# A new issue order, other engines for some copies and another warm-up table, in a recurrence followed by two dense layers

## The chip, the cores and the metric

One core of a Trainium2 chip runs the kernel. The metric is the device time of one execution in microseconds. Three runs of the kernel before gave 346.52, 346.58 and 348.45 us; the median is 346.58 us.

In the profile PE is TensorE (matmuls; PEld is its weight loads), DVE is VectorE, ACT is ScalarE, POOL is GpSimd, and SP is the engine that issues all transfers from memory.

## The reference

A recurrence over 768 positions (2 batches, 8 heads of 48 channels), then two dense layers:

```
for t in range(S):
    cur = einsum(u * k_t, v_t)                  # 48 x 48 per head
    y[t] = einsum(r_t, state + cur)
    state = w_t * state + einsum(k_t, v_t)
x = y as (2, 768, 384)
h = relu(x @ w_in)                              # 384 -> 1024
x = (h * sigmoid(conv over 3 positions of h)) @ w_out
out = x + relu(layernorm(x) @ w_ch1) @ w_ch2    # 384 -> 1536 -> 384
```

All data are float32; the weights arrive as 64-bit floats and are converted in the kernel.

## The kernel before

**Stages.** The recurrence is cut into 12 chunks of 64 positions. For chunk c the steps are:

- transfers `load_pk`, `load_kr`, `load_v` (decay, keys and queries, values);
- DVE scans `pa1` (L447) and `pa2` (L464) with a reciprocal `par` (L455) between them; the products `pak` (kd, L459) and `pa3` (xr, L475), on DVE or POOL; `pa5`, `bo1` on ACT;
- TensorE step `p1` (a_ps, kdn_ps), its copies `bo4` (bb, L514, ACT), `k2` (kdn, L479) and the masked product `bo5` (db, L517, DVE or POOL);
- TensorE step `p2`, then `a2` (db, L530, DVE), then TensorE step `p3` (y_ps, st_ps; it reads the values);
- `s2` (L548, DVE) and `s3` (ss, L479) update the state that `p2` of the next chunk reads; `y2` (L579, ACT) and `y3` (L583, DVE) copy the output away into xh, as a high and a low part; `p2` of the next chunk waits for `y3` as well.

Each p step is 32 to 64 small matmuls with as many weight loads.

The first dense layer works on four blocks i of 192 positions. `y4(i)` moves some rows of xh by DMA; `h1(i,f)` is 9 matmuls for one of 8 column groups f; ACT, DVE and POOL apply relu, convolution (`g2`, L635, two DVE instructions for each f) and gate (`g6p` on DVE or POOL); `o1(i,t,part)` is 6 matmuls for the second product. Block 0 can start when `y3(3)` and `y4(0)` are done. The last layer (`m1x`, `n1`) follows in three groups.

Weights are converted beside this: `vl` loads, `va` (ACT, L751) and twice `vc` (DVE, L761 and L766) build the float, `vh` and `vlo` split it into two parts. The last layer has `wl`, `wa`, `wc`, `wh`, `wlo`.

**What sets the order.** `PLACE` gives each of some 1,250 steps a number; steps are issued in that order, and each engine takes its own in that order and waits at the first that isn't ready. `ENGINE` says by a letter for each instance which engine does a step that can run on two (V is DVE, P is POOL, A is ACT). `WARM` puts matmuls without use (L957) ahead of the step with that number: `{10: 13}` puts 13 ahead of number 10. What each step computes is the same in both kernels.

```
for k in sorted(steps, key=place.get):
    if place[k] in WARM:
        order.append(("warm", WARM[place[k]]))
    order.append(k)
```

Of the kernel before, what the change touches and what calls it, by code (L numbers as in the profile page):

```python
# [48 lines left out]
    'init': (1,),  # L49
    'init_p': (0, 12),  # L50
    'load_cst': (7,),
    'load_cw': (82,),
    'load_gln': (125,),
    'top_a': (309,),
    'top_v': (429,),
    'conv_cw': (95,),
    'load_kr': (4, 19, 30),
    'load_pk': (2, 9, 29, 52, 91, 116, 163, 222, 278, 336, 384, 422),
# [50 lines left out]
    'free_attention': (525,),  # L109
    'wl': (531, 535, 554, 567, 583, 611, 631, 642, 659, 671, 688, 725, 729, 760, 782, 821, 841, 856, 876, 889,  # L110
        897, 909, 938, 956),
    'wa': (536, 549, 562, 579, 605, 621, 636, 655, 674, 693, 706, 732, 746, 805, 827, 835, 854, 864, 886, 895,
        915, 929, 952, 964),
    'wc': (541, 548, 555, 556, 571, 572, 581, 586, 612, 615, 629, 630, 640, 650, 657, 663, 675, 683, 696, 702,
        710, 719, 736, 742, 768, 772, 806, 817, 832, 833, 847, 849, 855, 860, 874, 875, 887, 892, 896, 906, 920,
        921, 940, 945, 953, 958, 970, 973),
# [1146 lines left out]
```

## Time and profile before

| | before |
|---|---|
| median of 3 runs | 346.58 us |
| profiled execution, its own time | 347.53 us |
| span of the profiled execution | 345.7 us |
| TensorE busy / VectorE busy / ScalarE busy / GpSimd busy | 318.4 / 216.9 / 252.4 / 117.2 us |
| mean granted TensorE clock | 0.968 |

The span runs from the first to the last instruction of one execution; its own time is 1.8 us longer. Busy shares are means over stages, so a stage is read on its own: by the busy time of each engine in it, and by what ended the waits in it.

### The profile page before, as it was taken

How to read it: one execution, taken by the hardware profiler on the slowest of the kernel's cores; microseconds unless marked ns; L12 is line 12 of the kernel's file. 1: busy time of each engine (PE TensorE's matmuls, PEld its weight loads, DVE VectorE, ACT ScalarE, POOL GpSimd, SP SyncE). 2: the span in 40 equal slices, each digit the busy share in tenths (PEclk: the TensorE clock that was granted, in tenths of full speed). 3: DMA queues.
4: the chain of work that ended last, by engine and by line, in shares of the span. 5: the costliest groups of instructions: out<-in, count | busy, mean ns of one | idle time of the engine just before them, and what ended most of it. 6: DMA issues, size and time to landing. Idle time of an engine off the chain costs nothing.

```text
span 345.7 us, 9057 instructions
## 1 busy us (share of the span) xinstructions
PE 318.4 (92%) x3611; PEld 284.7 (82%) x3619; DVE 216.9 (63%) x433; ACT 252.4 (73%) x664; POOL 117.2 (34%) x124
## 2 busy tenths in 40 slices
PE   7474697988999999999999999999999999999994
PEld 3453666868999889999988889899888999988994
DVE  7796799997998869988997837732423302142011
ACT  3463449987859466998998989867697868585960
POOL 3443438888448564497743211200000000000000
PEclk9969579999999999999999999999999999999998
DMA  7864668374144304544411433316546464363541
GB/s 236 329 238 144 236 187 276 101 266 131 36 156 144 84 2 138 137 141 126 138 46 50 134 92 92 93 46 166 155 109 173 133 203 121 75 196 88 177 114 37
DMA packets 16845, 47.91 MB, mean 139 GB/s; under 512 B 2720, under 2 KB 4512, under 8 KB 16800
## 3 DMA queue, kind: packets, MB, share of 16 engines
q1 hardware_dynamic: 16800, 47.31, 44.3%
q8 instruction: 29, 0.48, 0.6%
q14 instruction: 16, 0.13, 0.1%
HBM read 43.75 MB, written 2.36 MB: 133 GB/s over the span
## 4 chain that ended last, share of the span: by engine, by line
PE 61%; DVE 18%; ACT 7%; issue 6%; POOL 4%; DMA 2%; SPq 0%; ACTq 0%; DVEq 0%; POOLq 0%
PE h_ps L907 22%; PE o_b L924 11%; PE o_a L924 11%; DVE h_ps L635 5%; PE o_b L679 4%; PE h_ps L614 3%; PE a_ps L484 2%; PE y_ps L540 2%; PE o_a L679 2%; PE y_ps L525 2%; DVE stf L766 1%; DVE q L447 1%; DVE pp L464 1%; DMA pk<-in_pk 1%; ACT h_ps L632 1%
## 5 line engine op out<-in xcount | busy, mean ns | idle before, releaser
L907 PE MATMUL h_ps<-xh,w_s 128*128 128x512 f32 x324 | 79.0, 396 | 0.0
L907 PEld LDWEIGHTS h_ps<-xh,w_s 128*128 128x128 f32 x324 | 60.3, 188 | 12.4
L614 PE MATMUL h_ps<-xh,win_s 128*128 128x388 f32 x288 | 57.1, 345 | 1.3 <-ACT z L660 1.0
L614 PEld LDWEIGHTS h_ps<-xh,win_s 128*128 128x128 f32 x288 | 50.0, 188 | 3.8 <-ACT z L660 3.1
L635 DVE SCALAR_TENSOR_TENSOR h_ps<-h,cw_sb,h_ps 128x384 f32<-128x384 f32 x64 | 39.1, 614 | 3.4 <-ACT h_ps L632 2.3
L663 POOL TENSOR_TENSOR z<-z,h 128x384 f32<-128x384 f32 x32 | 32.6, 1021 | 22.4 <-ACT z L660 22.2
L916 DVE SCALAR_TENSOR_TENSOR win_s<-h_ps,win_s 128x512 fp32r<-128x512 f32 x18 | 12.4, 689 | 34.2 <-ACT win_s L913 34.2
L916 DVE SCALAR_TENSOR_TENSOR wout_s<-h_ps,wout_s 128x512 fp32r<-128x512 f32 x18 | 12.2, 689 | 28.6 <-ACT wout_s L913 28.5
L679 PE MATMUL o_b<-wout_s,gs 128*128 128x384 f32 x144 | 29.2, 342 | 0.0
L679 PE MATMUL o_a<-wout_s,gs 128*128 128x384 f32 x144 | 28.6, 340 | 0.0
L773 POOL TENSOR_TENSOR w_s<-stf,w_s 128x384 fp32r<-128x384 f32 x17 | 17.4, 1029 | 31.4 <-ACT w_s L770 21.8
L679 PEld LDWEIGHTS o_b<-wout_s,gs 128*128 128x128 f32 x144 | 25.0, 188 | 0.6
L679 PEld LDWEIGHTS o_a<-wout_s,gs 128*128 128x128 f32 x144 | 25.0, 188 | 0.4
L671 POOL TENSOR_TENSOR gs<-z,gs 128x384 fp32r<-128x384 f32 x20 | 20.7, 1038 | 13.3 <-ACT gs L667 13.2
L924 PE MATMUL o_b<-w_s,wout_s 128*128 128x384 f32 x108 | 20.8, 339 | 0.0
L924 PE MATMUL o_a<-w_s,win_s 128*128 128x384 f32 x108 | 20.7, 338 | 0.0
L924 PE MATMUL o_b<-w_s,win_s 128*128 128x384 f32 x108 | 20.5, 338 | 0.0
L660 ACT ACTIVATE z<-h_ps 128x384 f32<-128x384 f32 x32 | 15.8, 492 | 6.5 <-DVE h_ps L635 3.4
L924 PE MATMUL o_a<-w_s,wout_s 128*128 128x384 f32 x108 | 20.4, 339 | 0.0
L913 ACT ACTIVATE win_s<-h_ps 128x512 fp32r<-128x512 f32 x18 | 10.8, 599 | 13.2 <-PE h_ps L907 10.6
L507 PE MATMUL kdn_ps<-ident,kd 48*64 48x48 f32 x352 | 14.3, 232 | 6.4 <-issue 5.1
L459 POOL TENSOR_TENSOR kd<-pk,q 112x512 f32<-112x512 f32 x9 | 11.9, 1322 | 23.7 <-DVE q L447 11.4
(120 smaller groups left out, 730.4 us busy)
## 6 DMA issues: line engine op xcount, KB each, us to landing
stg<-in_w SPq DMA_DIRECT2D x36, 384.0 KB, 3.1
pk<-in_pk SPq DMA_DIRECT2D x9, 800.0 KB, 4.5
vs<-in_vn SPq DMA_DIRECT2D x12, 384.0 KB, 6.0
stg<-in_win SPq DMA_DIRECT2D x4, 768.0 KB, 7.2
stg<-in_wout SPq DMA_DIRECT2D x4, 768.0 KB, 5.6
stg<-in_win SPq DMA_DIRECT2D x8, 384.0 KB, 3.2
stg<-in_wout SPq DMA_DIRECT2D x8, 384.0 KB, 3.3
stg<-in_wf SPq DMA_DIRECT2D x6, 384.0 KB, 3.4
```

The costliest lines, as they stand in the source:

```text
L459: eng.tensor_mul(kd, gx(pk_t[c][0:112, KO:KO + 512], C), gx(q_t[c][:, 1:521], 65)[:, :, 1:65])
L507: PE.matmul(kp[lo:lo + 64, g, :], kd[lo:lo + 48, g, :], ident[lo:lo + 48, lo:lo + 48], start=True, stop=True)
L614: PE.matmul(hv, win_s[:, wa, m, kt, fs], x[:, kt, xa, :, 0:NX[i]], start=(k == 0), stop=(k == 8))
L635: V.scalar_tensor_tensor(out=z3(zp(i, f)), in0=tap(i, f, j), scalar=cw_sb[:, f, j:j + 1], in1=z3(zp(i, f)), op0=ALU.mult, op1=ALU.add)
L660: A.activation(z, zp(i, f), AF.Sigmoid)
L663: P.tensor_mul(z3(z_t[i, f]), z3(z_t[i, f]), tap(i, f, 1))
L671: eng.tensor_sub(gs[:, 1], z_t[i, f], _as_f32(gs[:, 0]))
L679: PE.matmul(op, g_t[i, f][:, ga, t * 128:(t + 1) * 128], wout_s[:, wa, f // 2, f % 2, :], start=(f == 0 and k == 0), stop=(f == MF - 1 and ...
L773: eng.tensor_sub(lo, f_t[key], _as_f32(hi))
L907: PE.matmul(hp, late["w1"][:, wa, m // 2, kt, (m % 2) * 128:(m % 2 + 1) * 128], xt(gr)[:, xa, kt].rearrange("p a t -> p (a t)"), start=(k ...
L916: V.scalar_tensor_tensor(out=h2s(m)[:, 1], in0=hp2_t[m], scalar=0.0, in1=_as_f32(h2s(m)[:, 0]), op0=ALU.max, op1=ALU.subtract)
L924: PE.matmul(op2_t[t], h2s(m)[:, ga, t * 128:(t + 1) * 128], late["w2"][:, wa, m // 2, m % 2, :], start=(m == 0 and k == 0), stop=(m == MF2 ...
```

## The change

The same steps with the same operands are issued in another order (`PLACE`), some instances change their engine (`ENGINE`), and the useless matmuls stand elsewhere and are 60 instead of 41 (`WARM`). The table of the pk buffers is filled beforehand, so that `load_kr` of a chunk may stand ahead of its `load_pk`.

```diff
-    'load_v': (20, 49, 83, 97, 124, 188, 273, 274, 386, 400, 423, 485),
+    'load_v': (23, 46, 73, 89, 153, 180, 229, 254, 321, 344, 434, 456),
...
-    'a2': (25, 59, 84, 108, 150, 224, 272, 321, 396, 450, 482, 513),
+    'a2': (28, 61, 92, 118, 159, 231, 282, 332, 405, 447, 481, 520),
...
-ENGINE = {'pak': 'PVPPPPVPPPVP',
-          'pa3': 'VPPPPPPPPPPP',
-          'bo1': 'AAAAAAAAAAAA',
-          'bo5': 'PPVVVPPPVVPP',
-          'k2': 'AVAAAAAAAAV',
-          's3': 'AAAVAAAAAAA',
-          'vlo': 'PPPPVPPV',
-          'g6p': 'PPPVPVVVVVVPPPVPPPPVPPPPPPVPVPVP',
-          'wlo': 'PVVPPPPPPPPPPVVPPPPVVPPV'}
...
-WARM = {10: 13, 55: 2, 60: 5, 85: 1, 107: 1, 111: 1, 143: 12, 202: 2, 266: 4}
+ENGINE = {'pak': 'VPPPPPPPVVPP',
+          'pa3': 'VVPPPPPPPPPP',
+          'bo1': 'AAAAAAAAAVAA',
+          'bo5': 'VPVPVPPVPPPP',
+          'k2': 'VAAAAAAVAAA',
+          's3': 'AAVAAAAVVAV',
+          'vlo': 'PPPPVPVP',
+          'g6p': 'VPPPPVPPPVPPPPPPPPPPPPPPVPVPPPPP',
+          'wlo': 'PVPPPPVPPPPVPPPPPPPPPVPV'}
...
+WARM = {15: 10, 37: 12, 44: 2, 58: 3, 85: 4, 96: 7, 113: 2, 123: 1, 144: 10, 157: 5, 211: 4}
...
-    pk_t = {}
+    pk_t = {c: pk_bufs[c % 2] for c in range(NCH)}
...
-        t = pk_t[c] = pk_bufs[c % 2]
+        t = pk_t[c]
```

Three places of the order are shown. The first is VectorE between `a2(2)` and `a2(3)`: from the two `vc` that follow `a2(2)` to `a2(3)` (L530) in the kernel before.

```order
L761 SCALAR_TENSOR_TENSOR o_b<-stg,o_b 128x384
L766 SCALAR_TENSOR_TENSOR stf<-stg,o_b 128x384
L548 TENSOR_TENSOR st_ps<-st_ps,wt 112x384
L790 TENSOR_SCALAR o_b<-cw_raw 128x24
L792 SCALAR_TENSOR_TENSOR o_b<-cw_raw,o_b 128x24
L793 SCALAR_TENSOR_TENSOR o_b<-cw_raw,o_b 128x24
L794 COPY cw_sb<-o_b 128x24
L583 TENSOR_TENSOR xh<-y_ps,xh 112x2x4x64
L583 TENSOR_TENSOR xh<-y_ps,xh 112x2x4
L517 TENSOR_TENSOR db_101<-bb,msk 128x512
L447 SCALAR_TENSOR_TENSOR q<-pk_98,ind 112x521
L530 COPY_PREDICATED db_101<-msk,a_ps 128x512
```

The same stretch of VectorE in the changed kernel, from the first instruction after `a2(2)` to `a2(3)`:

```order
L447 SCALAR_TENSOR_TENSOR q<-pk_98,ind 112x521
L761 SCALAR_TENSOR_TENSOR o_b<-stg,o_b 128x384
L548 TENSOR_TENSOR st_ps<-st_ps,wt 112x384
L766 SCALAR_TENSOR_TENSOR stf<-stg,o_b 128x384
L583 TENSOR_TENSOR xh<-y_ps,xh 112x2x4x64
L583 TENSOR_TENSOR xh<-y_ps,xh 112x2x4
L479 COPY ss<-st_ps 112x384
L455 RECIPROCAL d_0_102<-q 112x8
L761 SCALAR_TENSOR_TENSOR o_b<-stg,o_b 128x384
L766 SCALAR_TENSOR_TENSOR stf<-stg,o_b 128x384
L530 COPY_PREDICATED db_101<-msk,a_ps 128x512
```

The masked product `bo5(3)` (L517), which waits for ScalarE's copy of `p1(3)`, has left VectorE for GpSimd; the copy `s3(2)` has come, `pa1(4)` stands first instead of last, and two more `vc` stand ahead of `a2(3)`; the four small instructions of `conv_cw` stand earlier, ahead of `a2(2)`.

The second place is VectorE between `a2(3)` and the end of `y3(3)`, before:

```order
L455 RECIPROCAL d_0_102<-q 112x8
L761 SCALAR_TENSOR_TENSOR o_b<-stg,o_b 128x384
L464 SCALAR_TENSOR_TENSOR pp<-pk_98,d_0_102 112x520
L766 SCALAR_TENSOR_TENSOR stf<-stg,o_b 128x384
L583 TENSOR_TENSOR xh<-y_ps,xh 112x2x4x2
L583 TENSOR_TENSOR xh<-y_ps,xh 112x2x4x64
```

And in the changed kernel:

```order
L464 SCALAR_TENSOR_TENSOR pp<-pk_98,d_0_102 112x520
L761 SCALAR_TENSOR_TENSOR o_b<-stg,o_b 128x384
L766 SCALAR_TENSOR_TENSOR stf<-stg,o_b 128x384
L583 TENSOR_TENSOR xh<-y_ps,xh 112x2x4x2
L583 TENSOR_TENSOR xh<-y_ps,xh 112x2x4x64
```

Only `par(4)` has left the stretch; the two `vc` now belong to a later weight tile.

The third place is SP's queue of transfers, from the second chunk's `load_pk` on, before:

```order
L429 DMA pk1_99<-in_pk 128x522
L432 DMA pk1_99<-in_pk 128x1024
L435 DMA vs0_96<-in_vn 128x768
L737 DMA stg_221<-in_win 128x768
L429 DMA pk0_98<-in_pk 128x522
L432 DMA pk0_98<-in_pk 128x1024
L435 DMA vs1_97<-in_vn 128x768
```

And in the changed kernel:

```order
L429 DMA pk1_99<-in_pk 128x522
L432 DMA pk1_99<-in_pk 128x1024
L737 DMA stg_129<-in_win 128x768
L432 DMA pk0_98<-in_pk 128x1024
L429 DMA pk0_98<-in_pk 128x522
L435 DMA vs0_96<-in_vn 128x768
L783 DMA cw_raw_218<-in_cw 128x24
```

The values of the first chunk (vs0) are issued after a weight tile and after chunk 2's two parts of pk0, instead of ahead of them.

## Rows read from the trace of the kernel before

**Rows 1.** Page, part 1: busy us (share of span) xinstructions of each engine.

```profile
PE 318.4 (92%) x3611; PEld 284.7 (82%) x3619; DVE 216.9 (63%) x433; ACT 252.4 (73%) x664; POOL 117.2 (34%) x124
```

**Rows 2.** Page, part 2: tenths busy, and granted clock, in 40 equal slices of 8.64 us.

```profile
PE   7474697988999999999999999999999999999994
...
DVE  7796799997998869988997837732423302142011
...
PEclk9969579999999999999999999999999999999998
```

**Rows 3.** Busy us of each engine in five stretches, then granted clock, DMA share, GB/s.

```profile
0.00:43.62 43.62, 27.06 (x818) 20.21 (x823) 32.77 (x60) 19.43 (x51) 17.76 (x20) 0.80 0.66 234
43.62:72.98 29.36, 26.08 (x476) 20.18 (x475) 29.01 (x49) 24.57 (x59) 19.81 (x22) 0.94 0.64 203
72.98:81.63 8.65, 6.94 (x268) 6.17 (x268) 7.39 (x14) 6.14 (x17) 6.99 (x7) 1.00 0.49 168
81.63:340.85 259.22, 258.13 (x2061) 238.02 (x2053) 146.56 (x309) 202.22 (x541) 72.60 (x77) 1.00 0.40 116
340.85:345.70 4.85, 0.19 (x2) 0.09 (x2) 1.21 (x5) 0.00 (x0) 0.00 (x0) 0.82 0.15 49
```

**Rows 4.** VectorE in order of time, 5 to 46 us: start, us, instruction, [idle before <-releaser].

```profile
6.48 1.49 DVE L475 TENSOR_TENSOR xr<-pk,pp 112x512 f32<-112x512 f32 x1
...
10.54 0.72 DVE L530 COPY_PREDICATED db<-msk,a_ps 128x512 f32<-128x512 uint32 x1 [1.42 <-POOL db L517]
...
17.26 0.56 DVE L479 COPY kdn<-kdn_ps 128x384 f32<-128x384 f32 x1 [0.99 <-PE a_ps L484]
...
34.50 0.69 DVE L517 TENSOR_TENSOR db<-bb,msk 128x512 f32<-128x512 f32 x1 [2.64 <-ACT bb L514]
...
42.85 0.77 DVE L583 TENSOR_TENSOR xh<-y_ps,xh 112x16 fp32r<-112x16 f32 x2 [1.78 <-ACT xh L579]
```

**Rows 5.** Chain of waits, 0 to 50 us: start, us, what; TensorE's own breaks.

```profile
14.16 2.31 issue
...
26.51 0.66 issue
...
30.29 2.81 issue
...
38.96 2.06 issue
```

**Rows 6.** Page, part 3: DMA queue, kind, packets, MB, share of 16 engines.

```profile
q8 instruction: 29, 0.48, 0.6%
```

**Rows 7.** DMA queues within 30.29 to 33.09 us: packets, MB, share of 16 engines.

```profile
q8 instruction: 1, 0.02, 2.1%
q1 hardware_dynamic: 8, 0.02, 1.4%
```

**Rows 8.** VectorE's groups, 0 to 110 us: line, shapes, count | busy, mean ns | idle.

```profile
L464 DVE TENSOR_TENSOR_SCAN pp<-pk,d 112x520 f32<-112x520 f32 x11 | 15.4, 1398 | 0.2
L761 DVE SCALAR_TENSOR_TENSOR o_b<-stg,o_b 128x384 int32<-128x384 int32 x16 | 8.8, 553 | 1.1 <-ACT o_b L751 1.0
...
L548 DVE TENSOR_TENSOR st_ps<-st_ps,wt 112x384 f32<-112x384 f32 x9 | 5.0, 559 | 0.8 <-PE y_ps L540 0.8
...
L455 DVE RECIPROCAL d<-q 112x8 f32<-112x8 f32 x11 | 2.2, 197 | 0.1
L459 DVE TENSOR_TENSOR kd<-pk,q 112x512 f32<-112x512 f32 x3 | 2.1, 715 | 0.0
...
L479 DVE COPY ss<-st_ps 112x384 f32<-112x384 f32 x1 | 0.6, 551 | 0.0
```

**Rows 9.** Chain of waits: steps of TensorE and ScalarE that follow each other undisturbed.

```profile
25.07 0.60 ACT bb L514
...
42.21 0.61 ACT xh L579
...
117.97 1.04 PE o_a L679 x6
...
124.17 1.08 PE a_ps L484 x32
```

**Rows 10.** SP's queue in order of time: start, us to issue, transfer.

```profile
4.12 0.43 SPq L435 DMA_DIRECT2D vs<-in_vn  x1
...
8.68 0.33 SPq L432 DMA_DIRECT2D pk<-in_pk  x1
9.06 0.43 SPq L435 DMA_DIRECT2D vs<-in_vn  x1
```

**Rows 11.** Page, part 6: issues, count, KB each, median us to landing.

```profile
vs<-in_vn SPq DMA_DIRECT2D x12, 384.0 KB, 6.0
```

**Rows 12.** TensorE in order of time, around 44 us: useless matmuls at the lower clock.

```profile
44.15 3.95 PE L957 MATMUL o_a<-x 128*128 128x512 bf16 x11 [0.33 <-issue]
```

More of the change, by code (lines that the diff above doesn't have):

```diff
@@ L48 @@
 PLACE = {
[L49 to L58, printed above, removed]
-    'load_v': (20, 49, 83, 97, 124, 188, 273, 274, 386, 400, 423, 485),
-    'pa1': (3, 24, 35, 64, 103, 127, 172, 246, 312, 367, 394, 468),
-    'par': (13, 26, 45, 70, 109, 140, 200, 265, 328, 371, 413, 475),
@@ L62 @@
-    'pak': (6, 33, 37, 71, 117, 139, 212, 264, 323, 380, 431, 478),
[21 rows of a table removed]
-    'vlo': (99, 128, 151, 153, 247, 281, 314, 332),
[24 rows of a table removed]
[L109 to L116, printed above, removed]
@@ L117 @@
-    'wh': (550, 560, 597, 613, 620, 641, 658, 672, 685, 708, 743, 781, 792, 829, 839, 858, 865, 878, 913, 910,
-        943, 961, 963, 975),
-    'wlo': (568, 582, 610, 618, 644, 648, 679, 680, 701, 728, 744, 801, 823, 843, 853, 866, 867, 899, 919, 925,
[18 rows of a table removed]
-    'check': (745, 763, 764, 791, 797, 798, 810, 814, 816, 836, 838, 844, 846, 871, 872, 881, 884, 890, 891,
[7 rows of a table removed]
-    'load_ck': (983, 980, 992, 1004, 1007, 1015, 1026, 1032, 1042, 1048, 1057, 1073, 1079, 1084, 1096, 1104,
-        1106, 1110, 1121, 1126, 1130, 1137, 1146, 1154, 1164, 1175, 1180, 1194, 1200, 1212, 1213, 1221, 1225,
-        1233, 1244),
@@ L149 @@
-    'fl1': (1250,),
-    'fl2': (1251,),
-    'fl3': (1252,),
-}
-ENGINE = {'pak': 'PVPPPPVPPPVP',
-          'pa3': 'VPPPPPPPPPPP',
-          'bo1': 'AAAAAAAAAAAA',
-          'bo5': 'PPVVVPPPVVPP',
-          'k2': 'AVAAAAAAAAV',
-          's3': 'AAAVAAAAAAA',
-          'vlo': 'PPPPVPPV',
-          'g6p': 'PPPVPVVVVVVPPPVPPPPVPPPPPPVPVPVP',
-          'wlo': 'PVVPPPPPPPPPPVVPPPPVVPPV'}
-WARM = {10: 13, 55: 2, 60: 5, 85: 1, 107: 1, 111: 1, 143: 12, 202: 2, 266: 4}
+    'init': (4,),
+    'init_p': (1, 3),
@@ new lines @@
+    'load_cst': (5,),
+    'load_cw': (26,),
+    'load_gln': (376,),
+    'top_a': (360,),
+    'top_v': (490,),
+    'conv_cw': (90,),
+    'load_kr': (2, 7, 19),
+    'load_pk': (0, 6, 20, 43, 71, 107, 132, 177, 251, 317, 373, 432),
+    'load_v': (23, 46, 73, 89, 153, 180, 229, 254, 321, 344, 434, 456),
+    'pa1': (8, 17, 38, 65, 95, 140, 156, 208, 308, 353, 401, 471),
+    'par': (10, 25, 45, 72, 111, 150, 167, 240, 314, 388, 413, 477),
+    'pak': (12, 24, 41, 67, 115, 146, 173, 284, 348, 375, 419, 505),
[21 rows of a table added]
@@ new lines @@
+    'vlo': (75, 99, 131, 164, 224, 265, 302, 320),
[24 rows of a table added]
+    'free_attention': (527,),
+    'wl': (528, 530, 554, 564, 583, 606, 627, 648, 661, 680, 698, 715, 737, 763, 789, 815, 835, 847, 864, 890,
+        898, 914, 931, 946),
+    'wa': (539, 555, 571, 590, 604, 631, 647, 668, 686, 699, 719, 742, 772, 800, 817, 836, 855, 863, 879, 901,
+        919, 930, 948, 959),
+    'wc': (544, 550, 559, 562, 576, 580, 595, 600, 611, 622, 634, 644, 652, 659, 671, 674, 691, 695, 702, 711,
+        723, 732, 746, 759, 775, 784, 805, 810, 820, 832, 839, 843, 858, 860, 866, 868, 882, 887, 903, 910, 922,
+        923, 940, 942, 951, 954, 961, 968),
@@ new lines @@
+    'wh': (556, 585, 596, 607, 642, 656, 675, 679, 703, 726, 748, 795, 812, 828, 837, 848, 874, 881, 906, 917,
+        941, 947, 967, 972),
+    'wlo': (572, 593, 616, 621, 649, 667, 688, 685, 708, 739, 766, 807, 816, 831, 853, 850, 877, 885, 909, 920,
[18 rows of a table added]
+    'check': (758, 767, 777, 787, 792, 803, 808, 830, 842, 844, 856, 859, 861, 869, 871, 886, 889, 892, 896,
[7 rows of a table added]
+    'load_ck': (977, 978, 988, 991, 1003, 1008, 1018, 1025, 1037, 1049, 1053, 1064, 1073, 1080, 1089, 1096,
+        1102, 1110, 1115, 1125, 1134, 1140, 1147, 1158, 1163, 1174, 1179, 1189, 1195, 1205, 1209, 1218, 1223,
+        1232, 1237),
@@ L166 @@
+    'fl1': (1247,),
+    'fl2': (1249,),
+    'fl3': (1251,),
+}
+ENGINE = {'pak': 'VPPPPPPPVVPP',
[8 more added lines that the diff above has]
+WARM = {15: 10, 37: 12, 44: 2, 58: 3, 85: 4, 96: 7, 113: 2, 123: 1, 144: 10, 157: 5, 211: 4}
 EVC = NCH
```

138 rows, old and new, of the table PLACE are left out of this document.

## The prediction

> **What bounds the kernel now.** Start with the busy shares [rows 1]: TensorE is busy 92% of the span, no other engine over 73%. The slices [rows 2] show where the missing 8% lies: TensorE has sevens and fours in the first ten slices and nines from there to the end. The table by stretches [rows 3] puts numbers to it. I cut it where something ends: at 43.62 us (y3(3), the last thing that the first dense layer needs from the recurrence, but for the small transfers y4(0)), at 72.98 (y3(5), which releases p2(6)), at 81.63 (the end of p2(7)), at 340.85 (the last n1). TensorE idles 43.62 - 27.06 = 16.56 us in the first stretch, 29.36 - 26.08 = 3.28 in the second, 1.71 in the third, 1.09 in the fourth, though that lasts 259 us. So from about 82 us on TensorE is the bound, its work there is fixed, and the end moves with the amount of TensorE work that is already done at 82 us. The question for this change is how early TensorE gets there.
>
> What keeps TensorE waiting up to there is VectorE. In the second stretch it is busy 29.01 of 29.36 us, so that stretch lasts as long as VectorE's steps in it. In the first it is busy 32.77 of 43.62 and idles 10.85. Four places make 6.83 us of that [rows 4]: 1.42 us for POOL's bo5(0) ahead of a2(0), 0.99 for p1(1), 2.64 for ACT's copy of p1(3) ahead of bo5(3), 1.78 for y2(3), which follows p3(3). The rest is the start and small gaps.
>
> Three of the four have the same cause. The chain of waits has breaks of 2.31, 0.66, 2.81 and 2.06 us, together 7.84, in which TensorE stops in the middle of a step and waits for nothing that the profile shows ("issue") [rows 5]: in p1(1), p2(2), p1(3), p3(3). TensorE's instructions arrive over a DMA queue of their own, 29 packets and 0.48 MB, some 16 KB each [rows 6]. In the break at 30.29 us that queue moves one packet while the data queue is nearly empty (1.4%) [rows 7]: I read it as TensorE waiting for its next piece of code. A p step holds 64 to 128 instructions in about 1.1 us, an h1 step 18 in 1.8, which is why the breaks stand where p steps follow each other closely.
>
> [...]
>
> **The change, term by term.** No step is added but 19 useless matmuls; steps move, and some change engine.
>
> First stretch, VectorE's work up to the end of y3(3). The changed order has four more vc ahead of it (4 x 0.55), one xr more (pa3(1), 0.72 by the product of the same shape) and the copy s3(2) (0.55) [rows 8]; pak(0) for pak(1), k2(0) for k2(1) and bo5(0) for bo5(3) cancel. That is +3.47 us. Against it, xr of chunk 0 took 1.49 us [rows 4], twice the 0.72 of such a product alone [rows 8], beside a POOL product, kd, which is now VectorE's own: -0.77.
>
> First stretch, VectorE's waits. For each I compare what VectorE now has to do in the meantime with the time that the other engines need.
> - bo5(0) is now done by VectorE itself: the 1.42 us go, filled with a step that was counted above.
> - Between a2(0) and s2(0) stand k2(0), pa2(1), four vc, pa1(2), pa3(1) and par(2): 0.55 + 1.40 + 2.20 + 1.40 + 0.72 + 0.20 = 6.5 us [rows 8], from 11.26 us (the end of a2(0) in rows 4) to 17.7. In that time TensorE does p1(1) and p3(0). The values of chunk 0 are now issued behind chunk 2's pk0 and kr: not at 4.12 but about where those of chunk 1 were, 9.06 [rows 10], and land 6.0 later [rows 11], at 15.1. Then p3(0), 1.08 [rows 9], at 16.2, or at 19.0 with a break of 2.81 in it. Wait: 0 to 1.3.
> - Between a2(2) and a2(3): pa1(4), vc, s2(2), vc, y3(2), s3(2), par(4), two vc, 1.40 + 0.55 + 0.56 + 0.55 + 0.77 + 0.55 + 0.20 + 1.10 = 5.7 us. TensorE and ACT do p3(2), p1(3), bb and p2(3): 1.08 + 1.08 + 0.60 + 1.08 = 3.84 [rows 9], or 6.65 with a break. Wait: 0 to 1.0, in place of 2.64.
> - Between a2(3) and y3(3): pa2(4) and two vc, 2.5 us, beside p3(3) and y2(3), 1.08 + 0.61 = 1.7, or 3.75 with the break of 2.06 there. Wait: 0 to 1.3, in place of 1.78.
>
> So 0 to 3.6 us of waits stand against 6.83. I take the middle, 1.8, since nothing says that breaks vanish, only that some fall where VectorE has work: 5.0 saved. y3(3) ends at 43.62 - 5.0 - 0.77 + 3.47 = 41.3, that is 2.3 earlier.
>
> Second stretch, VectorE's work from there to the end of y3(5). It has two vc less, one ss and one kd less, and pa2(7) and par(7) more: -1.10 - 0.55 - 0.72 + 1.40 + 0.20 = -0.8 us. VectorE was saturated here [rows 3] and 12 of the 16 g2 of block 0 stay in it, so the stretch shortens by that. y3(5) is 3.1 us earlier.
>
> TensorE's work by then. Ahead of p2(6) the orders hold the same p and h1 steps, but the changed one has o1(0,0,0) too, 1.04 us [rows 9]. Third stretch: between p3(6) and p2(7) five o1 and p1(7) now stand where one o1 and p1(7) stood, so TensorE's 1.71 us of idleness there may go; I count nothing, since the o1 need VectorE's and POOL's low parts in time.
>
> The useless matmuls. A row of 11 at the lower clock took 3.95 us, 0.36 each [rows 12]; 19 more are at most 6.8 us on TensorE, which idles 16.56 in this stretch. The two big new groups are covered: 12 ahead of p1(1) (4.3 us at most, from p2(0)'s end near 10.4) stand before p3(0), which has to wait for its values until 15.1 anyway; 7 ahead of p3(2) (2.5) stand beside pa2(3) and conv_cw, which now precede a2(2). [...]
>
> After 82 us the steps are the same, and TensorE's idleness there, 1.09 us, leaves nothing to gain. VectorE and ACT are busy 147 and 202 us of 259 [rows 3], which leaves room for starting 4 us earlier. The tail of 4.85 us stays.
>
> Sum: 2.3 + 0.8 + 1.04 = 4.1 us. The profiled execution's span of 345.7 becomes 341.6, its own time of 347.53 becomes 343.4. That execution lies 0.95 us over the median of the runs, 346.58, from which I subtract the same: **342.5 us**, 1.2% faster.
>
> **Bounds.** Best: no wait is left (6.83 + 0.77 - 3.47 = 4.1), with 0.8, 1.04 and all of the 1.71: 7.7 us, 338.9. Worst without a new wait: all of the old waits return in other places and xr finds another POOL product beside it: -3.47 + 0.8 + 1.04 = -1.6, 348.2.
>
> **Rivals.**
> 1. *The waits stay with VectorE.* The breaks belong to the number of instructions, which even grows by 38; if each new break meets a VectorE that has run out of work, the added 3.47 us are simply longer: 348.2, or between there and 344 if half is kept. For it: the p steps of the first four chunks follow each other as closely as before. Against it: the fills of 6.5, 5.7 and 2.5 us. [...]
> 2. *Everything is hidden.* The breaks fall into the waits for VectorE, and TensorE finds o1 work in the third stretch: 338.9 to 340.6.
> 3. *Slower, by the late values of chunk 0.* p3(0) followed a2(0) at about 11.3; now it waits for values until 15.1, and if a break comes on top, it ends at 19.0. Then s2(0) and y3(0), and with them p2(1), come near 20.4 instead of 18.5 (y3(0) followed p1(1)'s copy of 17.26 in rows 4), 1.9 us later, and if the waits further on are as before, the time is 348.2 + 1.9 = 350.1. It decides if p3(0) ends after 17.7, the end of VectorE's fill. For it: the queue order, and a full data queue in that part. Against it: the break needs to fall behind the landing.
>
> **How the numbers follow.** Forecast, 340.6 to 344: 0.46. Rival 2: 0.15. Rival 1, 344 to 348.3: 0.27. Rival 3 and worse: 0.12. A measurement of this kernel can't tell less than about 1%, 3.5 us, from no change, so faster means below 343.1: rival 2 and some 0.38 of the forecast, 0.53. Slower means above 350.0: 0.12. The rest, 0.35, is the same. The range from 338.3 to 348.3 leaves out rival 3, the part of rival 1 that borders on it, and what is better than every bound.
>
> **What would show it.** In the changed profile: y3(3) ends near 41 us and VectorE idles under 7 us before it; the waits of 2.64 and 1.78 for ACT's copies are under 1.3 each; TensorE's breaks without a releaser are still there, but VectorE is busy beside them; y3(5) ends near 70 us, and p2(6) starts with o1(0,0,0) done; the long stretch to the last n1 has about as little idle time as before. I am wrong if VectorE idles 9 us or more before y3(3), if s2(0) comes after 18 us, or if TensorE, having got there earlier, waits for low parts or converted weights between 82 and 180 us.

## The result: slower, by one held instruction

The changed kernel takes 351.64 us (median of 4 runs, 349.88 to 351.81), the kernel before beside it 347.15 (4 runs): ratio 1.0114 [1.0079, 1.0148]. The forecast was 342.5, with a range up to 348.3. The profiled execution has a span of 350.0 us and an own time of 351.81, at the same mean clock of 0.968 as before. Of the times further down, the ten of `e_gap` include one slow run of 396.9 us (mean clock 0.75) and the profiled execution of `e_warm`, 351.38 us, counts as slow too; the ratios are formed without such runs.

The page's busy times first (busy us, share, count), which answer to [rows 1], and TensorE, VectorE and the clock in 40 slices, now of 8.75 us, which answer to [rows 2]:

```profile
PE 323.4 (92%) x3628; PEld 288.0 (82%) x3638; DVE 217.4 (62%) x428; ACT 250.4 (72%) x657; POOL 125.3 (36%) x133
...
PE   7777698939999999999999999999999999999995
...
DVE  7879979988798678879996667732333221221101
...
PEclk9969969978999999999999999999999999999998
```

The second and the fourth slice are fuller than before, with 7 instead of 4. The ninth, 70.0 to 78.8 us, is new: TensorE has a 3 there and the clock is down to 7 and 8 in that slice and the next. The table by stretches (length, then busy us and instructions of PE, PEld, DVE, ACT, POOL, granted clock, DMA share, GB/s) shows the same, with the cuts of [rows 3] and the last one moved to the last n1:

```profile
0.00:43.62 43.62, 31.66 (x904) 21.39 (x913) 37.51 (x74) 24.32 (x62) 19.09 (x22) 0.92 0.78 266
43.62:72.98 29.36, 25.06 (x424) 21.33 (x416) 26.93 (x35) 20.86 (x50) 20.64 (x23) 0.88 0.58 197
72.98:81.63 8.65, 5.20 (x132) 4.89 (x133) 6.20 (x13) 4.90 (x11) 2.48 (x2) 0.61 0.01 2
81.63:345.00 263.37, 260.78 (x2181) 240.01 (x2181) 146.19 (x308) 200.30 (x536) 83.07 (x87) 1.00 0.39 115
```

In the first stretch VectorE gets through 74 instructions instead of 60 and idles 43.62 - 37.51 = 6.1 us instead of 10.85. In the second it does 35 instead of 49, and yet counts as busy 26.93 us: a sign of an instruction that takes long without doing more. From 73 to 82 us TensorE is busy 5.20 of 8.65 us, at a clock of 0.61.

VectorE in order of time, 0 to 46 us (start, us, instruction, [idle before <-releaser]); the longest waits of [rows 4] and what is left of them:

```profile
7.00 0.69 DVE L475 TENSOR_TENSOR xr<-pk,pp 112x512 f32<-112x512 f32 x1
...
17.02 0.56 DVE L548 TENSOR_TENSOR st_ps<-st_ps,wt 112x384 f32<-112x384 f32 x1
...
24.97 0.57 DVE L548 TENSOR_TENSOR st_ps<-st_ps,wt 112x384 f32<-112x384 f32 x1 [1.40 <-PE y_ps L540]
...
35.47 0.73 DVE L530 COPY_PREDICATED db<-msk,a_ps 128x512 f32<-128x512 uint32 x1 [0.27 <-PE a_ps L484]
```

The product xr of chunk 0 takes 0.69 us, s2(0) starts at 17.02, and the wait of 2.64 us ahead of chunk 3's turn is 0.27. y3(3) ends at 39.05 us; before it was 43.62. In the chain of waits up to 45 us TensorE's breaks without a releaser [rows 5] are gone: its own waits without one are now at most 0.3 us each. The longest "issue" left in the chain are these (start, us, what):

```profile
31.92 0.44 issue
...
35.56 0.53 issue
...
37.84 0.44 issue
```

Now VectorE from 66 to 76 us:

```profile
66.57 0.56 DVE L548 TENSOR_TENSOR st_ps<-st_ps,wt 112x384 f32<-112x384 f32 x1
67.03 6.63 DVE L464 TENSOR_TENSOR_SCAN pp<-pk,d 112x520 f32<-112x520 f32 x1
73.59 0.53 DVE L761 SCALAR_TENSOR_TENSOR o_b<-stg,o_b 128x384 int32<-128x384 int32 x1
74.16 0.56 DVE L766 SCALAR_TENSOR_TENSOR stf<-stg,o_b 128x384 int32<-128x384 int32 x1
74.63 0.77 DVE L583 TENSOR_TENSOR xh<-y_ps,xh 112x512 fp32r<-112x512 f32 x2
```

And GpSimd at the same time:

```profile
66.49 0.86 POOL L663 TENSOR_TENSOR z<-z,h 128x384 f32<-128x384 f32 x1
67.30 0.09 POOL L604 MEMSET h<- 128x2 f32 x1
67.36 1.85 POOL L773 TENSOR_TENSOR wout_s<-stf,wout_s 128x768 fp32r<-128x768 f32 x1
69.13 0.11 POOL L604 MEMSET h<- 128x2 f32 x1
69.19 1.29 POOL L517 TENSOR_TENSOR db<-bb,msk 128x512 f32<-128x512 f32 x1
70.43 1.00 POOL L671 TENSOR_TENSOR gs<-z,gs 128x384 fp32r<-128x384 f32 x1
71.38 1.19 POOL L459 TENSOR_TENSOR kd<-pk,q 112x512 f32<-112x512 f32 x1
72.51 1.81 POOL L663 TENSOR_TENSOR z<-z,h 128x384 f32<-128x384 f32 x1
```

The scan pa2(7) (L464) reads two operands in SBUF and takes 6.63 us; in the kernel before the same instruction took 1.24. It starts inside g4p(0,4) on GpSimd, a product of two SBUF operands, and such products then follow each other without a gap: vlo(wout,1), bo5(6), g6p(0,4), pak(7). The scan ends at 73.67; 1.24 us earlier, 72.43, is about where pak(7) ends (72.57), and the next product, g4p(0,5), takes 1.81 instead of 0.86. So I read the 6.63 us as 5.4 of waiting and 1.24 of work, after which GpSimd waited in its turn.

It is not the only scan that is held. pa1(6), which took 1.24 us in the kernel before, takes 2.66 beside the product vlo(win,3) of 46.07 to 47.89 on GpSimd:

```profile
46.33 2.66 DVE L447 TENSOR_TENSOR_SCAN q<-pk,ind 112x521 f32<-112x521 f32 x1 [1.54 <-DMA pk<-in_pk]
```

Behind pa2(7) in VectorE's order stands y3(5), which ends at 75.39, and p2(6) on TensorE waits for it (start, us, instruction, [idle before <-releaser]):

```profile
69.14 1.20 PE L679 MATMUL o_a<-wout_s,gs 128*128 128x384 f32 x6
75.54 0.35 PE L525 MATMUL y_ps<-xr,ss 48*48 48x64 f32 x2 [5.20 <-POOL xr L475]
```

The releaser named in this row is wrong: GpSimd's xr of 74.29 to 75.46 belongs to the next chunk and only happens to end last. What fits in every kernel here is y3(5): p2(6) starts 0.14 to 0.15 us after its end (72.98 and 73.12 before, 75.39 and 75.54 here), and in `e_scan` below p2(6) starts 3.8 us ahead of that xr.

The traces of the two kernels show which VectorE instructions are held like this scan. In their first 200 us, vc and s2, which read one of their operands from PSUM, keep to 0.52 to 0.58 and 0.55 to 0.57 us, also beside GpSimd's products. Of those that read two operands from SBUF, the scans go from 1.24 us to 6.63 and 2.66 here and to 2.46 in the kernel before, and bo5 goes from 0.68 to 2.63 there. What makes one engine wait for the other, no trace shows. Four products, vlo(wout,1) to pak(7), began while the scan stood there with its 6.63 us; I read it as VectorE being passed over several times in a row.

### The profile page after: what moved, and what is told of

The parts are those of the page before. It is cut to its first block, busy times and chain, and to the rows that moved or that the text cites. A ratio compares the mean times of both kernels' runs of the same rounds, so it can differ in the third digit from the quotient of the medians.

```text
span 350.0 us, 9090 instructions
## 1 busy us (share of the span) xinstructions
PE 323.4 (92%) x3628; PEld 288.0 (82%) x3638; DVE 217.4 (62%) x428; ACT 250.4 (72%) x657; POOL 125.3 (36%) x133
## 4 chain that ended last, share of the span: by engine, by line
PE 65%; DVE 12%; ACT 8%; DMA 6%; POOL 5%; issue 3%; SPq 0%; DVEq 0%; ACTq 0%; POOLq 0%
PE h_ps L907 21%; PE o_b L924 11%; PE o_a L924 11%; PE h_ps L614 6%; PE o_b L679 5%; PE o_a L679 3%; DVE h_ps L635 3%; PE a_ps L484 3%; DMA vs<-in_vn 2%; DMA xh<-xh 2%; POOL z L663 2%; DMA pk<-in_pk 2%; PE y_ps L540 1%; ACT h_ps L632 1%; PE o_a L957 1%
## 5 line engine op out<-in xcount | busy, mean ns | idle before, releaser
L614 PE MATMUL h_ps<-xh,win_s 128*128 128x388 f32 x288 | 58.7, 354 | 3.3 <-ACT z L660 2.6
L614 PEld LDWEIGHTS h_ps<-xh,win_s 128*128 128x128 f32 x288 | 51.8, 194 | 7.2 <-ACT z L660 5.0
L663 POOL TENSOR_TENSOR z<-z,h 128x384 f32<-128x384 f32 x32 | 31.3, 983 | 36.5 <-ACT z L660 25.8
L671 POOL TENSOR_TENSOR gs<-z,gs 128x384 fp32r<-128x384 f32 x27 | 28.3, 1059 | 7.5 <-ACT gs L667 5.2
L773 POOL TENSOR_TENSOR w_s<-stf,w_s 128x384 fp32r<-128x384 f32 x19 | 19.7, 1039 | 30.1 <-ACT w_s L770 29.9
L679 PE MATMUL o_a<-wout_s,gs 128*128 128x384 f32 x144 | 30.1, 346 | 0.0
L525 PEld LDWEIGHTS y_ps<-xr,ss 48*48 48x48 f32 x352 | 11.6, 128 | 13.5 <-issue 5.5
L619 ACT ACTIVATE h<-h_ps 128x388 f32<-128x388 f32 x32 | 15.7, 493 | 9.4 <-PE h_ps L614 9.4
L525 PE MATMUL y_ps<-xr,ss 48*48 48x64 f32 x352 | 13.3, 228 | 9.4 <-POOL xr L475 5.2
```

The source lines that it names most:

```text
L525: PE.matmul(y_ps[lo:lo + 48, g // 4, g % 4, :], ss_t[c - 1][lo:lo + 48, g, :], xr[lo:lo + 48, g, :], start=(g == 0), stop=True, skip_group ...
L614: PE.matmul(hv, win_s[:, wa, m, kt, fs], x[:, kt, xa, :, 0:NX[i]], start=(k == 0), stop=(k == 8))
L619: A.activation(h_t[i, f][:, :, c0:c0 + NX[i]], hp_t[i, f][:, 0:B * NX[i]].rearrange("p (b t) -> p b t", b=B), AF.Relu)
L663: P.tensor_mul(z3(z_t[i, f]), z3(z_t[i, f]), tap(i, f, 1))
L671: eng.tensor_sub(gs[:, 1], z_t[i, f], _as_f32(gs[:, 0]))
L679: PE.matmul(op, g_t[i, f][:, ga, t * 128:(t + 1) * 128], wout_s[:, wa, f // 2, f % 2, :], start=(f == 0 and k == 0), stop=(f == MF - 1 and ...
```

## The experiments

A place in the table `PLACE` is a sort key: a step with a higher number is issued later on its engine. Theory A was that the held scan is the loss, with the low clock behind it as a consequence. The rivals were B, that GpSimd itself is late or overloaded there, and C, that the loss is the late start of the first dense layer, h1(0,0) at 46.63, which waits for the transfers y4(0). Theory F was about [rows 5]: whether TensorE's breaks are set by where the pieces of its code begin. In the sessions of these experiments the median of the kernel before was 346.50 to 346.64 us.

**`e_gap`: one step out of GpSimd's train.**

```diff
-    'vlo': (75, 99, 131, 164, 224, 265, 302, 320),
+    'vlo': (75, 99, 131, 164, 224, 276.5, 302, 320),
```

> The changed kernel with one POOL step, vlo(wout,1), moved behind bo5(6), so that POOL has to wait for ScalarE's copy of p1(6) between g4p(0,4) and bo5(6). Theory A (VectorE's scan pa2(7) is kept waiting 5.4 us because POOL runs five products of two SBUF operands without a pause): the scan takes 1.2 to 1.9 us instead of 6.63, y3(5) ends near 70.3 us instead of 75.4, TensorE's gap of 5.09 us before p2(6) shrinks to under 1, the clock stays at 1.00 from 73 to 82 us, and the time falls from 351.6 to 343 to 346. Rival B (POOL has too much work, and p2(6) waits for its product xr, as the wait list names it): POOL's work is the same, the gap stays at 4 to 5 us and the time within 1 us of 351.6.

Measured: 344.66 us (10 runs), ratio to before 0.9938 [0.9899, 0.9978]. VectorE, then GpSimd, at the same place:

```profile
66.09 1.43 DVE L464 TENSOR_TENSOR_SCAN pp<-pk,d 112x520 f32<-112x520 f32 x1
...
68.65 0.77 DVE L583 TENSOR_TENSOR xh<-y_ps,xh 112x512 fp32r<-112x512 f32 x2
```

```profile
65.56 0.86 POOL L663 TENSOR_TENSOR z<-z,h 128x384 f32<-128x384 f32 x1
...
67.67 1.30 POOL L517 TENSOR_TENSOR db<-bb,msk 128x512 f32<-128x512 f32 x1 [1.10 <-ACT bb L514]
68.93 1.84 POOL L773 TENSOR_TENSOR wout_s<-stf,wout_s 128x768 fp32r<-128x768 f32 x1
```

GpSimd now has a gap of 1.10 us ahead of bo5(6), and the scan runs in it: 1.43 us. y3(5) ends at 69.42, p2(6) starts at 69.57, and the window from 73 to 82 us is full and at full clock:

```profile
72.98:81.63 8.65, 8.65 (x172) 7.95 (x165) 8.25 (x15) 5.02 (x14) 5.82 (x5) 1.00 0.39 95
```

Moving one product on an engine that is busy 36% takes 7.0 us off the median, 6.1 by the two ratios. The account closes: p2(6) starts 75.54 - 69.57 = 5.97 us earlier, the steps from there to the start of p2(7) take 79.81 - 69.57 = 10.24 us instead of 87.61 - 75.54 = 12.07, so p2(7) comes 7.80 earlier, and the span is 350.0 - 342.1 = 7.9 shorter. Not all of the 5.97 us are this scan's: it is 5.20 us shorter, and it starts 0.94 us earlier, 66.09 instead of 67.03, though the order up to there is the same. In the changed kernel's execution the granted clock was 0.59 from 46 to 52 us and the first two h1 steps took 5.40 us; in that of `e_gap` it was 1.00 and they took 3.47. A holds, B doesn't: GpSimd does the same work and is later with vlo(wout,1). Nor does C: h1(0,0) starts at 46.16, hardly earlier than 46.63, and the loss is gone all the same.

**`e_scan`: the scan alone back behind y3(5).**

```diff
-    'pa2': (14, 30, 56, 87, 120, 154, 191, 258, 342, 395, 453, 486),
+    'pa2': (14, 30, 56, 87, 120, 154, 191, 271.5, 342, 395, 453, 486),
```

> The changed kernel with pa2(7) alone put back behind y3(5) in VectorE's order, as before the change; POOL's train of five products stays. Theory A (the gap of 5.1 us ahead of p2(6) is the held scan pa2(7) standing ahead of y3(5)): y3(5) ends near 70 and p2(6) starts near 70.3; the scan may still be held for 3 us or more by what is left of the train, and then a2(6) comes late behind it; time 345 to 348. Rival B (the gap comes from POOL's late steps themselves): p2(6) still starts after 74, time 351.6 within 1.

Measured: 347.29 us (10 runs), ratio 1.0024 [0.9993, 1.0056]. VectorE (first two rows, then a2(6)):

```profile
68.95 0.77 DVE L583 TENSOR_TENSOR xh<-y_ps,xh 112x512 fp32r<-112x512 f32 x2 [1.41 <-ACT xh L579]
69.64 3.43 DVE L464 TENSOR_TENSOR_SCAN pp<-pk,d 112x520 f32<-112x520 f32 x1
...
74.10 0.73 DVE L530 COPY_PREDICATED db<-msk,a_ps 128x512 f32<-128x512 uint32 x1
```

TensorE, p2(6) and p3(6):

```profile
69.87 0.26 PE L525 MATMUL y_ps<-xr,ss 48*48 48x64 f32 x2
...
74.88 0.26 PE L540 MATMUL y_ps<-db,vs 64*48 64x64 f32 x2 [3.85 <-DVE db L530]
```

The gap ahead of p2(6) is gone, with GpSimd's train as it was. The scan is still held, 3.43 us, until pak(7) ends, and a2(6) behind it makes TensorE wait 3.85 us ahead of p3(6). So the hold costs what stands behind the held instruction, and moving the victim passes a smaller part of it to the next step: 4.3 us won (3.1 by the ratios), where taking one product out of the train won 7.0 (6.1).

**`e_warm`: the clock's part.** 20 useless matmuls on a scratch PSUM tile, issued ahead of p2(6).

```diff
+    def keep(n):
+        t = ps.tile([128, G, C], F32, name="a_ps")
+        for _ in range(n):
+            PE.matmul(t.rearrange("p g c -> p (g c)"), wm[0][:, 0:128], wm[0], start=True, stop=True)
...
+            if k == ("p2", 6):
+                keep(20)
```

> The changed kernel with 20 more useless matmuls ahead of p2(6), where TensorE idles 5.09 us. Theory A, second half (the gap costs once more, since the clock falls to its lower level after it and p2(6), p3(6) and o1(0,0,1) take 2.0, 1.95 and 1.9 us instead of 1.15, 1.1 and 1.2): the scan still takes 6 to 7 us, p2(6) still starts near 75.5, the clock is 0.9 to 1.00 from 73 to 82 us instead of 0.61, and the time falls by 2 to 2.5 us to 349. Rival (these steps are not what the end waits for): 351.6 within 0.7.

Measured: 348.97 us (10 runs), ratio 1.0048 [1.0011, 1.0085]. The profiled execution is one of the longest of the ten, so its rows are read for the steps and not for the time. Its window from 73 to 82 us, where the changed kernel's clock was 0.61:

```profile
72.98:81.63 8.65, 6.95 (x153) 5.07 (x151) 7.87 (x15) 5.47 (x12) 3.43 (x3) 1.00 0.02 5
```

The scan is held as before (6.66 us), but p2(6) takes 1.16 us instead of 2.00, and from p2(6) to p2(7) it is 86.32 - 76.48 = 9.84 us instead of 12.07. So 2 to 2.7 us of the loss (2.3 by the ratios, whose intervals just touch) go with the lower clock after the long wait, the rest with the wait.

**`e_y4`: an earlier start of the first dense layer.** The transfers y4(0) ahead of load_pk(6) in SP's queue.

```diff
-    'load_pk': (0, 6, 20, 43, 71, 107, 132, 177, 251, 317, 373, 432),
+    'load_pk': (0, 6, 20, 43, 71, 107, 135, 177, 251, 317, 373, 432),
...
-    'y4': (135, 300, 463, 586),
+    'y4': (132, 300, 463, 586),
```

> The changed kernel with the small transfers y4(0) issued ahead of load_pk(6) instead of behind it. Rival C (the gain of the first stretch is lost in SP's queue: y3(3) ends at 39.05 but h1(0,0) starts at 46.63, since y4(0) lands 6.85 us late behind 800 KB): h1(0,0) starts near 44.5 us, and the time falls by about the same 2 us to 349.5. Theory A: h1(0,0) starts near 44.5 too, but VectorE is the bound there, so the time moves only with what the scans meet on POOL, somewhere from 346 to 352.

Measured: 352.51 us (4 runs), ratio 1.0147 [1.0083, 1.0212]. h1(0,0) starts at 42.73 instead of 46.63, and nothing comes of it: the scan takes 6.61 us, y3(5) ends at 75.52, p2(6) starts at 75.66. The chain of waits of the changed kernel runs through those transfers (39.74, 6.85 us), yet 3.9 us less there are 0 at the end. By itself this doesn't dispose of C, since load_pk(6) now comes later and VectorE waits 4.79 us for it, where it waited 1.54:

```profile
48.50 1.24 DVE L447 TENSOR_TENSOR_SCAN q<-pk,ind 112x521 f32<-112x521 f32 x1 [4.79 <-DMA pk<-in_pk]
```

What disposes of C is `e_gap`, with the start of h1(0,0) as late as ever.

**`e_gap2`: a second step out of the way.** Besides, vlo(win,3) behind pak(6), since pa1(6), a scan of two SBUF operands too, took 3.17 us beside it in `e_gap`.

```diff
-    'vlo': (75, 99, 131, 164, 224, 265, 302, 320),
+    'vlo': (75, 99, 131, 173.5, 224, 276.5, 302, 320),
```

> The changed kernel with vlo(wout,1) moved behind bo5(6) on POOL, and now vlo(win,3) moved behind pak(6) too, so that pa1(6) on VectorE has no POOL product of two SBUF operands beside it at its start. Theory A (a VectorE instruction that reads two SBUF operands is held while POOL runs such products): pa1(6) takes 1.24 to 1.5 us instead of 3.17, y3(5) ends 1.0 to 1.9 us before 69.42, and the time falls from 344.66 to 342.5 to 344. Rival B (VectorE is not what the end of this stretch hangs on): pa1(6) is shorter but y3(5) and the time stay, 344.7 within 0.7.

Measured: 343.31 us (4 runs), ratio 0.9886 [0.9838, 0.9933]. pa1(6) is 1.24 us:

```profile
45.51 1.24 DVE L447 TENSOR_TENSOR_SCAN q<-pk,ind 112x521 f32<-112x521 f32 x1 [1.47 <-DMA pk<-in_pk]
```

But y3(5) ends at 69.74, not before 69.42. The time fell as A expected and y3(5) did not, so both were timed again side by side:

> The same kernel as e_gap2 (both vlo steps moved on POOL), timed again in five rounds beside e_gap on one chip, since e_gap2 had four runs only. Theory A with VectorE still the bound: 343.3 within 0.7, that is 1 to 1.5 us under e_gap. Rival (y3(5) hangs on ScalarE's y2(5) in both, so the shorter pa1(6) gains nothing): equal to e_gap within 0.6.

> The same kernel as e_gap (only vlo(wout,1) moved behind bo5(6) on POOL), timed again beside e_gap2: 344.7 within 0.7 by both theories; what is to be seen is the difference to e_gap2_r.

Measured: `e_gap2_r` 343.13 us (6 runs), 0.9911 [0.9882, 0.994]; `e_gap_r` 343.71 (6 runs, 0.3 us under what was expected of it), 0.991 [0.9878, 0.9942]. Over these runs the second step is worth nothing that can be measured. The traces show what it does in single executions. From the end of y3(3) to the end of y3(5) it takes 30.38 us in `e_gap` and in `e_gap_r`, with pa1(6) at 3.17 and 3.71; 28.68 in `e_gap2_r`, with pa1(6) at 1.24; but 31.40 in `e_gap2`, where pa1(6) is 1.24 as well. What was lost again there are two waits of VectorE for ScalarE's h_ps, behind the first h1 steps, here in `e_gap2` and then in `e_gap2_r` (the same kernel):

```profile
49.70 1.28 DVE L635 SCALAR_TENSOR_TENSOR h_ps<-h,cw_sb,h_ps 128x384 f32<-128x384 f32 x2 [1.15 <-ACT h_ps L632]
...
52.68 0.62 DVE L635 SCALAR_TENSOR_TENSOR h_ps<-h,cw_sb,h_ps 128x384 f32<-128x384 f32 x1 [1.23 <-ACT h_ps L632]
```

```profile
48.91 1.28 DVE L635 SCALAR_TENSOR_TENSOR h_ps<-h,cw_sb,h_ps 128x384 f32<-128x384 f32 x2 [0.35 <-ACT h_ps L632]
...
51.38 0.62 DVE L635 SCALAR_TENSOR_TENSOR h_ps<-h,cw_sb,h_ps 128x384 f32<-128x384 f32 x1 [0.53 <-ACT h_ps L632]
```

From 46 to 52 us the granted clock is 0.72 in the execution of `e_gap2` and 1.00 in that of `e_gap2_r`, and the first two h1 steps take 5.34 and 3.58 us. So at full clock the second step shortens the stretch by 1.70 us, near what A expected, and a lower clock in the same stretch can take that back. The rival, that ScalarE's y2(5) holds y3(5) whatever pa1(6) takes, doesn't fit `e_gap2_r`: there y2(5) starts 27.15 us behind y3(3), in `e_gap` 28.81. How often the clock is low there, and so what the step is worth on average, stays open.

**`e_comb`: `e_gap2` with the earlier y4(0).** Both edits as above.

> e_gap2 with y4(0) also ahead of load_pk(6) in SyncE's order, which by itself gained nothing (352.51) although h1(0,0) came 3.9 us earlier. Theory A says that this was because the held scan set the end of the stretch. With the scan free, h1(0,0) at 43 instead of 46.2 gives TensorE 3 us in the second stretch, of which up to 2 can be used before VectorE's y3(5) binds again: 341.5 to 344, and not over e_gap2 by more than 0.3. Rival (VectorE's y3(5) binds in either case): equal to e_gap2 within 0.7, or 0.5 slower by the later load of chunk 6.

Measured: 345.14 us (12 runs), 0.996 [0.9928, 0.9992]. h1(0,0) at 42.77, y3(5) at 69.66, as in `e_gap2`; p2(7) at 81.60 instead of 80.15. That y3(5) stays is what the rival expected, and the later load that it names is in the trace: VectorE waits 4.06 us for chunk 6's pk, and pa1(6) starts at 48.02 instead of 45.51. The time is some 2 us over `e_gap2`, more than it allowed. In its profiled execution the clock of the window from 73 to 82 us is 0.83 with TensorE busy throughout; whether that is in all of its runs stays open.

**`e_back`: the converse.** The kernel before, with pa2(7) ahead of y3(5). In this kernel the scan stands ahead of par(7), so it reads the reciprocals of chunk 5, and chunk 7's results differ; instructions and sizes are the same.

```diff
-    'pa2': (14, 32, 53, 80, 112, 144, 220, 270, 345, 393, 448, 486),
+    'pa2': (14, 32, 53, 80, 112, 144, 220, 255, 345, 393, 448, 486),
```

> The converse: the kernel before with one step moved, pa2(7) on VectorE ahead of y3(5), as in the change. On POOL pak(7) (70.19 to 71.96) and bo5(6) (71.92 to 73.19) stand there, two products of two SBUF operands back to back. Theory A: the scan comes to its place near 71.3 to 71.9 and is held until 73.2, so it takes 2.4 to 3.2 us instead of 1.24; y3(5) ends at 75.2 to 75.8 instead of 72.98, and the time is 1 to 3 us over that of before, 347.5 to 349.5. Rival B (the order on VectorE alone costs 1.24 us and nothing is held): the scan takes 1.24, y3(5) ends at 74.2, the time is 346.5 to 347.8.

Measured: 347.7 us (9 runs), 1.003 [1.0012, 1.0048]. VectorE, then GpSimd:

```profile
71.76 1.38 DVE L464 TENSOR_TENSOR_SCAN pp<-pk,d 112x520 f32<-112x520 f32 x1
```

```profile
70.20 1.77 POOL L459 TENSOR_TENSOR kd<-pk,q 112x512 f32<-112x512 f32 x1 [1.71 <-PE h_ps L614]
71.92 2.28 POOL L517 TENSOR_TENSOR db<-bb,msk 128x512 f32<-128x512 f32 x1
```

A's expectation is missed, and it tells something. The scan came 0.2 us before the end of pak(7) and was next; it was bo5(6) that was held, 2.28 us instead of 1.26. y3(5) ends at 74.26, 1.28 later, as rival B says, by the scan's own length. In `e_gap2_r`, too, GpSimd is the one held: its xr takes 2.17 us instead of 1.17 beside pa1(6), which started 0.07 us ahead of it. So where two such instructions meet in these rows one of them takes longer, and it isn't always VectorE's: the scan with 6.63 and 3.43 us for 1.24 in the changed kernel and in `e_scan`, GpSimd's bo5(6) and xr here. In those two kernels the scan ends 1.1 us after pak(7), in `e_back` 1.2 us, which is about its own length; why it got in just there is open.

**`e_nudge` and `e_nudge24`: the breaks of the kernel before.** 16, then 24 useless 64-column matmuls at the start: with their weight loads 32 and 48 instructions that shift all the code behind them.

```diff
+    def nudge(n):
+        warm(0)
+        for _ in range(n):
+            PE.matmul(wm[1][:, 0:64], wm[0][:, 0:128], wm[0][:, 0:64], start=True, stop=True)
...
+        nudge(16)
```

> The kernel before with 16 small useless matmuls (64 columns) at its very start, while TensorE has nothing to do: they add 32 instructions, so every crossing into the next 16 KB of TensorE's code comes 32 instructions earlier in its step. Theory F (a break comes where the request for the next piece falls behind a wait, so that the crossing follows the request too closely; 32 instructions earlier the request falls ahead of the wait): the breaks in p1(1), p1(3) and p3(3), 2.31, 2.81 and 2.06 us, go or fall below 0.7 each, y3(3) ends at 39 to 41 us instead of 43.62, and the time falls from 347.2 to 343 to 346. Rival G (the breaks come from elsewhere, the data transfers or the waits around): they stay in the same steps with 7 to 8 us in all, and the time stays within 1 us of 347.2.

Measured: 345.07 us (10 runs), 0.9952 [0.9929, 0.9974]. Chain of waits, the breaks left:

```profile
26.11 0.60 issue
...
29.84 2.53 issue
```

> The kernel before with 24 instead of 16 useless 64-column matmuls at the start, 48 instructions instead of 32. Theory F (the breaks in TensorE's steps stand where its next piece of code was asked for too late, and the request goes out some 65 instructions after the last crossing, unless TensorE is held at a wait by then; 16 more instructions move that point ahead of the wait of p3(2)): the break of 2.53 us in p1(3), which stayed with 16, goes too, y3(3) ends at 39.0 to 40.5 instead of 41.12, and the time falls from 345.07 to 342.5 to 344.5. Rival (the position of the code decides nothing further, or other breaks appear elsewhere in the first 45 us): 345 within 1.

Measured: 344.71 us (11 runs), 0.9946 [0.9925, 0.9966]. The same place:

```profile
26.78 0.57 issue
...
30.70 2.82 issue
```

The expectation was met in part. With no edit but useless matmuls at the start, the breaks of 2.31 us in p1(1) and 2.06 in p3(3) [rows 5] are gone with 16, and y3(3) ends at 41.12 instead of 43.62; with 24, p1(1) has a break of 0.78 again and y3(3) ends at 42.38, where 39.0 to 40.5 was expected. The break in p1(3) stayed in both. A break belongs to a position of the code, not to the step: counted in the trace, the four breaks of before come behind TensorE's first 221, 475, 602 and 729 weight loads, that is 254, 127 and 127 apart, and those behind 475 and 602 come behind the same numbers in all three kernels, though the steps have moved by 16 and 24 loads. With a matmul to each load, 127 loads are 254 instructions; 7,230 instructions [rows 1] in 29 packets [rows 6] are 249 each; that those packets are TensorE's code, and the breaks the wait for them, is a reading from these counts. But the position doesn't decide alone, since two of the four breaks went or shrank. That the next piece is asked for some 65 instructions after the last crossing was an assumption of mine, which no run shows: by it the break in p1(3), 2.82 us with 24, would have gone. How the pieces are asked for stays open. So does how much of the gain is the breaks' own: from 40 to 44 and from 44 to 48 us the clock is 0.95 and 1.00 in `e_nudge`, where it was 0.50 and 0.62 in the kernel before.

## Why the prediction was wrong, step by step

- *What bounds the kernel.* Right: TensorE is the bound from about 82 us on, and the end moves with p2(7), 7.80 us against 7.9 of the span between the changed kernel and `e_gap`.
- *First stretch, "5.0 saved", y3(3) at 41.3.* Right in the waits, partly by luck: up to y3(3) VectorE idles 5.95 us instead of 10.85, 4.9 less. But the prediction let TensorE's breaks [rows 5] go on beside a busy VectorE, and they are gone, which it did not forecast; no run shows how much of the 4.9 the fills alone would have saved. y3(3) ends at 39.05 because of the other term, VectorE's work: 3.47 - 0.77 = 2.70 us more were forecast, and it is busy 33.10 us up to there instead of 32.77. The kernel before has two more held scans in this stretch, one of 1.76 us and this one, beside vlo on GpSimd; the changed kernel has none over 1.42 there:

```profile
38.17 2.46 DVE L464 TENSOR_TENSOR_SCAN pp<-pk,d 112x520 f32<-112x520 f32 x1
```

- *Rival 3, the late values of chunk 0.* Not decisive: p3(0) ends at 16.20, ahead of the 17.7 given as its point of decision, and s2(0) starts at 17.02.
- *Second stretch, "VectorE was saturated here [rows 3] and 12 of the 16 g2 of block 0 stay in it, so the stretch shortens by that", y3(5) near 69.9.* **This is the step that failed.** It entered pa2(7) with 1.40 us, the mean of its group [rows 8], and the instruction took 6.63. y3(5) ends at 75.39, 5.5 us later than forecast. Counted from y3(3) the miss is larger, 75.39 - 39.05 = 36.34 us instead of 28.6: 5.2 by pa2(7), 1.4 by pa1(6) with 2.66, the rest a balance of smaller terms. The number of steps in the stretch was right; what was not asked is what GpSimd does beside them. The prediction had the same effect in its hands: it explained xr's 1.49 us [rows 4] against 0.72 by a GpSimd product beside it, and stopped there. Nor did VectorE's busy time of 29.01 of 29.36 us [rows 3] mean work only: being held counts as busy, and in that stretch of the kernel before bo5(4) took 2.63 us beside two GpSimd products, where bo5(3) took 0.69 [rows 4]:

```profile
47.79 2.63 DVE L517 TENSOR_TENSOR db<-bb,msk 128x512 f32<-128x512 f32 x1
```

- *p2(6) with o1(0,0,0) done, 1.04.* The order came about (o1 at 69.14, p2(6) at 75.54), but it was worth nothing in front of a wait of 5.2.
- *Third stretch, counted as nothing.* It lost about 2: the clock after the wait, 0.61 from 73 to 82 us, by `e_warm` 2 to 2.7 us. With the 5.5 that makes 7.5 to 8.2 of the 351.81 - 343.4 = 8.4 us by which the profiled execution missed the forecast.
- *Useless matmuls, after 82 us.* Close to the forecast: TensorE idles 263.37 - 260.78 = 2.6 us in the long stretch (1.7 of them h1's waits for ScalarE), where it was 1.09 [rows 3], and a first stretch that gains more than forecast shows no sign of matmuls in the way.
- *The whole sum without the hold.* `e_gap` is that kernel but for one step: y3(5) at 69.42 against 69.9, a span of 342.1 against 341.6, medians of 344.66 and 343.71 against 342.5. That y3(5) lies so near the forecast is in part luck: the first stretch ended 2.3 us earlier than forecast, and the second took 30.38 us instead of 28.6, 1.9 of them the other held scan, pa1(6) with 3.17.
- *TensorE's breaks read as waiting for code [rows 5].* `e_nudge` speaks for a price of the code's position: 32 instructions at the start, with no step moved, were worth 1.4 us of the median, 345.07 against 346.50, and 2.5 us at y3(3).
- *Signs that the prediction listed.* Of the three that would have shown it wrong none came (VectorE idles 5.95 us before y3(3), s2(0) is at 17.02, the long stretch is full); of those that were to show it right, two failed, y3(5) near 70 and breaks that are still there. It was wrong at a place that it took to be safe, since it looked for waits there, and the 6.63 us of the held scan stand in the trace as busy time, not as a wait.

The best kernel of these runs is the change with one or two low-part products moved on GpSimd: `e_gap2`, 343.13 to 343.31 us against 346.52 to 346.64, 0.9911 [0.9882, 0.994] in the longer measurement.

## What to carry to other kernels

Where a change moves VectorE instructions that read two SBUF operands, or GpSimd's products, lay both engines' orders beside each other and look for rows of GpSimd instructions without a gap; here the price was what stood behind the held instruction, and moving a member of the row won 7.0 us where moving the victim won 4.3. Compare an instruction's longest with its shortest time in a group: a mean of 1.40 for a scan that takes 1.24, with a longest of 2.46, was the trace's warning. TensorE's wait of 5.2 us was paid twice here: once as the wait and once as the clock behind it, 0.61 from 73 to 82 us, 2 to 2.7 us by `e_warm`. And one profiled execution can carry a stretch of low clock that another of the same kernel doesn't, 0.72 against 1.00 from 46 to 52 us here: look at the clock before comparing two traces.
